# Fillers for TensorE at the head of a fused attention and two-layer kernel, with the order of the other work kept

## The chip, the core and the metric

The kernel runs on one core of a Trainium2 chip. The metric is device microseconds of one execution. Five engines work side by side, each in its own order: TensorE (matrix products, turns), VectorE, ScalarE and GpSimd (elementwise work), and SyncE, which here only issues DMA transfers. They wait for each other by semaphores.

## What is computed

Attention over 4 batches, 8 heads, 576 positions and 64 columns per head, with a rotation by position of q and k first; then two gated layers on the 2304 x 512 result. All in float32:

```python
q_rot, k_rot = rotate(q), rotate(k)            # x1*cos - x2*sin, x1*sin + x2*cos
scores = (1 / sqrt(64)) * q_rot @ k_rot.T
attn = exp(scores - max(scores)); attn /= attn.sum(-1) + 1e-9
x = (attn @ v), heads side by side              # 2304 x 512
h = (x @ w1) * (x @ w2) @ w3;  y = h @ w_out    # 512 -> 1024 -> 1024 -> 512
z = max(y @ v1, y @ v2, y @ v3) @ v_out         # 512 -> 768 -> 512
```

## The kernel before

The heads go in 16 pairs; the two heads of a pair, 64 columns each, fill the 128 partitions. For a pair, `prepare` (line 587) loads q and k with their swapped halves, multiplies them by the tables of cosines and sines, adds, and splits the result into a high and a low part of the tensor `st` (line 619), since most products are made of three products of parts in the faster float32r type. `prepare_v` does the same for the values. `score` (line 645) makes one block of scores of both heads: 12 products of 288 columns, or 6 for the block of the last 64 rows of both heads, which goes through one of two tiles `zs` that are zeroed at the start (line 582) and that pairs take in turn. Behind each block VectorE takes the row maximum (line 668) and ScalarE the exponential (line 671). `turn` (line 698) transposes blocks of 128 x 128 on TensorE by the identity matrix, which is loaded from DRAM into the tile `ident`; `fill` copies and subtracts the turned blocks into a high and a low part (lines 441 and 708), and `values` multiplies them with v. In the kernel before, the first instruction that reads `ident` is the first turn of pair 0.

Beside the pairs, weights that arrive as float64 words are loaded (`raw`), converted by ScalarE and VectorE (lines 506, 509, 511), and folded together (`fold`, plain float32 products); then the gates and the two layers follow, nearly all of it on TensorE.

Turns, values and folds take their PSUM banks from one set of four (`banks = Share(4)`): up to two tiles for turns, one for values, two for folds at a time.

The order of the work comes from a planner. Every piece is a task with an engine, a cost, a priority and its dependencies. `Plan.order` plays the tasks on a clock of its own, one per engine that starts at 0.7: of the tasks that are ready on an engine it takes the one with the least priority, lets the engine's clock wait for the task if it must, and adds the cost; loads have a modelled landing time. The order in which tasks are taken is the order in which their instructions are issued, engine by engine, and each engine runs its instructions in that order. The priorities written at each task are then shifted by 509 seeded random moves (`MOVES`), which also choose, where a task may run on either of two engines, which one.

Of the kernel before, what the change touches and what calls it, by code (L numbers as in the profile page):

```python
# [26 lines left out]

PN = (256, 320)
# [17 lines left out]
MOVES = (  # L46
# [50 lines left out]
def draws(seed):  # L97
    mask = (1 << 64) - 1
    s = (seed * 0xD1342543DE82EF95 + 1) & mask
    while True:  # L100
        s = (s + 0x9E3779B97F4A7C15) & mask
        z = ((s ^ (s >> 30)) * 0xBF58476D1CE4E5B9) & mask
        z = ((z ^ (z >> 27)) * 0x94D049BB133111EB) & mask
        yield z ^ (z >> 31)


def move(prio, pick, opts, place, seed):


    d = draws(seed)  # L110

    def uni():
        return (next(d) >> 11) * (1.0 / 9007199254740992.0)

    def stretch(parts):
        width = len(prio) / parts
        lo = uni() * (len(prio) + width) - width
        return lo, lo + width

    kind = next(d) >> 62  # L120
    if kind == 1:
        parts, share = (32, 128, 512, 2048)[next(d) >> 62], (0.03, 0.1, 0.3, 1.0)[next(d) >> 62]
        lo, hi = stretch(parts)
        for i in range(len(prio)):
            if opts[i] > 1 and lo <= place[i] < hi and uni() < share:
                pick[i] = int(uni() * opts[i])
        return
    if kind == 0:
        by, width = (0.3, 1.0, 3.0, 10.0)[next(d) >> 62], 1 << (next(d) >> 61)
        lo = int(uni() * (len(prio) + width)) - width  # L130
        x = uni() + uni() + uni() + uni() - 2.0
        for i in range(max(lo, 0), min(lo + width, len(prio))):
            prio[i] = prio[i] + by * 1.7 * x
        return
    by, share = (0.1, 0.3, 0.6, 1.5)[next(d) >> 62], (0.01, 0.03, 0.1, 0.3)[next(d) >> 62]
    parts = (1, 8, 32, 128)[next(d) >> 62]
    lo, hi = stretch(parts)
    if parts == 1:
        share *= 0.3
    for i in range(len(prio)):  # L140
        if lo <= place[i] < hi and uni() < share:
            x = uni() + uni() + uni() + uni() - 2.0
            prio[i] = prio[i] + by * 1.7 * x
# [1067 lines left out]
```

## Time and profile before

| | before |
|---|---|
| three runs | 926.47, 927.95, 928.65 us; median 927.95 |
| profiled execution, its own time | 927.38 us |
| its span, first to last instruction | 925.4 us |
| TensorE busy | 891.0 us (96%) |
| VectorE, ScalarE, GpSimd busy | 633.0, 475.9, 342.4 us |
| granted TensorE clock, mean | 0.998 |

Times in the rows are microseconds from the start of the span. PE is TensorE (PEld its loading of the stationary operand), DVE VectorE, ACT ScalarE, POOL GpSimd, SP SyncE, SPq its issuing of DMAs. A busy TensorE is not TensorE at its peak, since products are pipelined and their ends are modelled. L423 is the line of the product helper, L676 that of the turn, L444 that of the loads.

### The profile page before, as it was taken

What the parts mean: (1) busy time and instruction counts of PE and PEld (TensorE: products, weight loads), DVE (VectorE), ACT (ScalarE), POOL (GpSimd) and SP (SyncE); (2) the same over time, 40 slices, a digit from 0 to 9 for tenths busy, and PEclk for the clock granted to TensorE, in tenths of its full rate; (3) what the DMA queues carried; (4) which work ended last, traced back from release to release, by engine and by line L of the source; (5) the groups of instructions that cost most, each with busy time, mean ns of one, the idle gap of its engine ahead of it and who ended that gap; (6) DMA issues with size and microseconds to landing.
All of it is one profiled execution on the core that took longest, in us unless ns stands there. A gap on an engine that the chain in (4) does not pass through costs nothing.

```text
span 925.4 us, 16273 instructions
## 1 busy us (share of the span) xinstructions
PE 891.0 (96%) x5922; PEld 823.8 (89%) x5922; DVE 633.0 (68%) x1133; ACT 475.9 (51%) x1054; POOL 342.4 (37%) x332
## 2 busy tenths in 40 slices
PE   1898999999999999999999999999999999999998
PEld 1666769989999999999998999999999999999886
DVE  6997988898867677687766333657988577578300
ACT  4677887876757577567544222434323322334411
POOL 3645767766436366522110000433332333232000
PEclk9999999999999999999999999999999999999999
DMA  8454546542333123310147543323324114255511
GB/s 265 134 188 153 165 154 209 149 142 84 100 103 97 44 92 93 97 50 18 37 153 213 199 127 89 103 86 97 98 86 140 55 46 148 68 163 195 201 57 68
DMA packets 80287, 110.31 MB, mean 119 GB/s; under 512 B 27984, under 2 KB 61008, under 8 KB 80208
## 3 DMA queue, kind: packets, MB, share of 16 engines
q1 hardware_dynamic: 80208, 109.29, 37.4%
q8 instruction: 46, 0.75, 0.3%
q14 instruction: 33, 0.27, 0.1%
HBM read 83.76 MB, written 25.50 MB: 118 GB/s over the span
## 4 chain that ended last, share of the span: by engine, by line
PE 80%; DVE 9%; DMA 7%; issue 2%; ACT 1%; SPq 1%; POOL 0%; DVEq 0%; ACTq 0%
PE q L423 46%; PE m L423 15%; PE t L676 7%; PE pv L423 6%; PE s L423 6%; DVE pt L708 3%; DMA raw<-in_w3t_dram 3%; DVE sm L668 2%; DMA raw<-in_w_dram 2%; DVE raw L509 1%; DMA rawc<-in_w3t_dram 1%; SPq L444 1%; DMA vr<-in_vv_dram 1%; DVE cw L511 1%; ACT pt L441 0%
## 5 line engine op out<-in xcount | busy, mean ns | idle before, releaser
L708 DVE TENSOR_TENSOR pt<-t,pt 128x320 fp32r<-128x320 f32 (+3 forms) x256 | 132.4, 528 | 34.5 <-ACT pt L441 29.4
L441 ACT CAST pt<-t 128x320 fp32r<-128x320 f32 (+3 forms) x234 | 103.5, 456 | 51.9 <-PE t L676 24.9
L423 PE MATMUL pv<-pt,v 128*128 128x256 f32 (+1 forms) x576 | 113.2, 317 | 5.1 <-DVE pt L708 4.0
L668 DVE TENSOR_REDUCE sm<-s 128x1 f32<-128x576 f32 x144 | 103.9, 749 | 19.8 <-PE s L423 18.8
L423 PE MATMUL q<-gt,wp 128*128 128x384 f32 x576 | 100.0, 334 | 0.0
L423 PEld LDWEIGHTS q<-gt,wp 128*128 128x128 f32 x576 | 99.8, 188 | 0.0
L423 PEld LDWEIGHTS pv<-pt,v 128*128 128x128 f32 x576 | 82.8, 189 | 15.7 <-DVE pt L708 9.5
L423 PE MATMUL s<-st 64*128 64x288 f32 x768 | 71.7, 316 | 18.7 <-ACT st L618 11.7
L423 PEld LDWEIGHTS s<-st 64*128 64x128 f32 x768 | 55.6, 190 | 32.5 <-ACT st L618 11.7
L423 PE MATMUL q<-yc__7620,u 128*128 128x384 f32 x378 | 71.2, 340 | 0.0
L423 PE MATMUL q<-yc__7946,u 128*128 128x384 f32 x378 | 70.8, 340 | 0.0
L423 PE MATMUL q<-yc__7376,u 128*128 128x384 f32 x378 | 70.5, 340 | 0.0
L423 PEld LDWEIGHTS q<-yc__7946,u 128*128 128x128 f32 x378 | 67.1, 188 | 0.1
L423 PEld LDWEIGHTS q<-yc__7620,u 128*128 128x128 f32 x378 | 67.1, 188 | 0.0
L423 PEld LDWEIGHTS q<-yc__7376,u 128*128 128x128 f32 x378 | 67.1, 188 | 0.0
L441 ACT COPY tmp<-q 128x384 f32<-128x384 f32 x45 | 21.5, 479 | 84.7 <-PE q L423 84.5
L441 ACT COPY ga<-q 128x512 f32<-128x512 f32 (+2 forms) x34 | 16.9, 497 | 65.6 <-PE q L423 61.6
L1066 POOL TENSOR_TENSOR tmp<-tmp 128x384 f32<-128x384 f32 x20 | 22.6, 1132 | 72.3 <-ACT tmp L441 72.3
L423 PE MATMUL q<-tail,tail 128*128 128x512 f32 x216 | 49.1, 389 | 0.0
L423 PEld LDWEIGHTS q<-tail,tail 128*128 128x128 f32 x216 | 40.5, 188 | 8.4
L522 DVE TENSOR_TENSOR gt<-gt 128x768 fp32r<-128x768 f32 x24 | 26.7, 1117 | 25.3 <-ACT gt L521 25.3
L1079 DVE TENSOR_TENSOR tmp<-q,tmp 128x384 f32<-128x384 f32 x54 | 29.9, 554 | 15.4 <-PE q L423 15.2
(1222 smaller groups left out, 2050.9 us busy)
## 6 DMA issues: line engine op xcount, KB each, us to landing
gt<-g_d SPq DMA_DIRECT2D x24, 384.0 KB
raw<-in_m_dram SPq DMA_DIRECT2D x72, 128.0 KB
raw<-in_w_dram SPq DMA_DIRECT2D x16, 512.0 KB
h_d<-top SPq DMA_DIRECT2D x36, 192.0 KB
tail<-h_d SPq DMA_DIRECT2D x36, 192.0 KB
raw<-in_wo_dram SPq DMA_DIRECT2D x12, 512.0 KB
raw<-in_w3t_dram SPq DMA_DIRECT2D x12, 512.0 KB
g_d<-ga SPq DMA_DIRECT2D x32, 160.0 KB
```

The lines of the kernel that those rows point to most:

```text
L423: pe.matmul(o, a, b, start=start, stop=stop, **kw)
L441: (e.copy if e is act else e.tensor_copy)(o, i)
L444: return add("SP", .5, lambda: sync.dma_start(o(), src()), r, w, part, deps, prio, tail=us)
L509: add("DVE", 0.42, lambda: dve.tensor_scalar(low_word(), low_word(), 29, None, ALU.logical_shift_right), part=[raw], deps=raw.writers, pri ...
L511: add("DVE", 0.69, lambda: dve.scalar_tensor_tensor(u(), u(), 3, low_word(), ALU.logical_shift_left, ALU.bitwise_or), r=[raw], deps=[first ...
L522: either(sb(n, "DVE"), lambda on: on.tensor_tensor(sel()[:, LO], f32(sel()[:, LO]), f32(sel()[:, HI]), ALU.subtract), r=[dst], part=[dst], ...
L668: add("DVE", c_dve(S), lambda s=s, col=col: dve.tensor_reduce(sm.t[:, 0, col:col + 1], s.t[:, :, :288], axis=AX.XY, op=ALU.max, negate=Tru ...
L676: pe.transpose(o, x, ident.t)
L708: add("DVE", c_dve(n), lambda: dve.tensor_tensor(low(pt.t), src(t.t), f32(hi(pt.t)), ALU.subtract), r=[t], part=[pt], deps=[h], prio=prio)
L1066: either(sb(TN), lambda on: on.tensor_tensor(s5.t, s1.t, s5.t, ALU.add), r=[s1], w=[s5], prio=prio)
L1079: add("DVE", c_dve(TN), lambda: dve.tensor_tensor(e.t, at_(o), e.t, ALU.add), r=[accs[o]], w=[e], prio=prio)
```

## The change

- TensorE gets a task `early` of 22 plain float32 products of 128 x 128 x 128. They read the second `zs` tile, which a new memset fills with ones, and write a PSUM bank of their own; a further memset then sets the tile back to zero.
- Ahead of every TensorE task that finds a gap on the planner's clock, once that clock is past 10.0, the kernel issues turns of the identity into the same bank: 0.7 of the gap, divided by 0.109. This goes on until the last values product of pair 0 (`plan.last`, a task that issues nothing); until then the bank is held, one of the four. The turns cost nothing on the planner's clock.
- The moves are replaced by two tables: `PLACE`, one rank for each task, and `OTHER`, the tasks that take their second engine. Of the tasks that both kernels have, the ranks are those of the final priorities before. The four new tasks stand among them at 148 (ones), 27 (products), 293 (zeros) and 28 (the end).

```diff
--- before.py
+++ after.py
@@ -25,6 +25,7 @@
 FF = 1024
 EPS = 1e-9
 
+IDLE = 1
 PN = (256, 320)
 PO = (0, 256)
 TN = 384
@@ -43,108 +44,245 @@
 
 
 
-MOVES = (
-    10000024, 10000032, 10000048, 10000067, 10000110, 10000112, 10000169, 10000173, 10000183, 10000227, 10000237,
...
+PLACE = (
+    14, 15, 148, 27, 293, 16, 311, 24, 188, 258, 238, 259, 218, 256, 240, 118, 241, 216, 208, 198, 203, 129, 299,
...
 )
 
 
-def draws(seed):
...
-def move(prio, pick, opts, place, seed):
...
+OTHER = (
+    23, 24, 51, 60, 67, 146, 152, 155, 156, 188, 277, 286, 288, 348, 415, 417, 418, 527, 533, 556, 680, 800, 851,
...
+)
 
 
 class Task:
-    __slots__ = ("eng", "dur", "emit", "prio", "tail", "deps", "after", "out", "next", "fresh", "shared", "num", "lock", "opts")
+    __slots__ = ("eng", "dur", "emit", "prio", "tail", "deps", "after", "out", "next", "fresh", "shared", "num", "lock", "opts", "idle")
 
 
 class Buf:
@@ -184,6 +322,7 @@
     LAT = {"PE": 0.05, "ACT": 0.035, "DVE": 0.035, "POOL": 0.08, "SP": 0.1, "HOST": 0.0}
     LAP = {"PE": 0.0, "ACT": 0.1, "DVE": 0.08, "POOL": 0.04, "SP": 0.0, "HOST": 0.0}
     DRAIN = 0.165
+    HEAD, FILL = 22, 0.7
 
     def __init__(self):
         self.tasks, self.rings = [], []
@@ -200,7 +339,7 @@
         k.eng, k.dur, k.prio, k.tail = eng, dur, prio, tail
         k.lock = eng == "POOL" if lock is None else lock
         k.opts = [(eng, dur, k.lock)]
-        k.num, k.out, k.next = len(self.tasks), [], []
+        k.num, k.out, k.next, k.idle = len(self.tasks), [], [], 0
         need = set(deps)
         after, fresh = set(), []
         for b in r:
@@ -224,6 +363,7 @@
         k.shared = list({id(b): b for b in list(r) + list(w) + list(part) if b.ring.share}.values())
 
         def go():
+            self.ahead(k.idle)
             for b in fresh:
                 b.t = b.make(b.slot)
             emit()
@@ -250,6 +390,7 @@
         soon = {e: [] for e in clock}
         now = {e: [] for e in clock}
         dma, port, done = 0.0, 0.0, []
+        idle, idling = {}, True
         for k in tasks:
             if not left[k.num]:
                 heapq.heappush(soon[k.eng], (0.0, k.num))
@@ -286,6 +427,10 @@
                 live[b.ring] += 1
             if k.lock:
                 at = max(at, port)
+            if k is self.last:
+                idling = False
+            if e == "PE" and idling and clock[e] > 10.0:
+                idle[k] = max(0, int(self.FILL * (at - clock[e]) / 0.109))
             end = at + k.dur
             if k.lock:
                 port = end
@@ -319,7 +464,7 @@
                 left[o.num] -= 1
                 if not left[o.num]:
                     heapq.heappush(soon[o.eng], (ready[o.num], o.num))
-        return clock["PE"], done, slot
+        return clock["PE"], done, slot, idle
 
     def issue(self):
         for ring in self.rings:
@@ -338,16 +483,14 @@
                 d.out.append(k)
             for d in sorted(k.after, key=lambda d: d.num):
                 d.next.append(k)
-        prio = [k.prio for k in self.tasks]
-        place = {k.num: i for i, k in enumerate(self.order(prio)[1])}
-        pick = [0] * len(prio)
-        for seed in MOVES:
-            move(prio, pick, [len(k.opts) for k in self.tasks], place, seed)
+        other = set(OTHER)
         for k in self.tasks:
-            k.eng, k.dur, k.lock = k.opts[pick[k.num]]
-        best = self.order(prio)
+            k.eng, k.dur, k.lock = k.opts[k.num in other]
+        best = self.order(PLACE)
         for b, n in best[2].items():
             b.slot = n
+        for k, n in best[3].items():
+            k.idle = n
         for k in best[1]:
             k.emit()
 
@@ -451,6 +594,7 @@
     cw_r = ring(gap, [128, 512], F32, "cw", 2)
     banks = Share(4)
     m_r = ring(ps_m, [128, 512], F32, "m", 2, banks)
+    idle_r = ring(ps_m, [128, 512], F32, "idle", 1, banks)
     banks2 = Share(8)
     q_r = ring("ps2", [128, 512], F32, "q", 8, banks2, False)
     q2_r = ring("ps2", [128, 512], F32, "q", 8, banks2)
@@ -675,6 +819,23 @@
     def tr(o, x):
         pe.transpose(o, x, ident.t)
 
+    bank = idle_r.new()
+
+    def ahead(n):
+
+        for _ in range(n):
+            tr(bank.t[:, :128], ident.t)
+
+    def early():
+
+        for _ in range(plan.HEAD):
+            mm(bank.t[:, :128], f32(zs[1].t[:, 0]), f32(zs[1].t[:, 1]), True, True)
+
+    plan.ahead = ahead
+    add("POOL", 0.3, lambda: pool.memset(f32(zs[1].t), 1.0), part=[zs[1]], deps=zs[1].writers, prio=-1, lock=False)
+    plan.first = add("PE", 8.5, early, r=[zs[1]], w=[bank], prio=-9)
+    add("POOL", 0.3, lambda: pool.memset(f32(zs[1].t), 0.0), part=[zs[1]], deps=[plan.first], prio=0.5, lock=False)
+
     def inverse(p):
 
         sm, prio = sms[p], 2 * p + 2.3
@@ -801,6 +962,8 @@
         prepare(p)
         if p == 0:
             load(lambda: ident.t, lambda: cs[:, 2 * S:], 0.4, w=[ident], prio=-2)
+        if p == IDLE:
+            plan.last = add("PE", 0.0, lambda: None, r=[bank], deps=[vs[p - 1].users[-1]], prio=-9)
         sms[p], xs[p] = sm_r.new(), [r.new() for r in x_r]
         prepare_v(p)
         for part in range(2):
```

## Rows read from the trace of the kernel before

**Rows 1.** by stretch: each engine's busy us, granted TensorE clock, DMA share, GB/s

```profile
27.00:38.00 11.00, 8.73 (x65) 6.92 (x64) 10.81 (x20) 7.98 (x19) 5.42 (x4) 1.00 0.25 69
77.40:130.00 52.60, 51.46 (x326) 36.27 (x326) 45.01 (x84) 44.83 (x109) 33.07 (x28) 1.00 0.57 170
```

**Rows 2.** chain that ended last, by time: start us, us, what

```profile
20.26 1.59 PE s L423 x9
21.88 0.77 DVE sm L668
23.64 1.79 PE s L423 x6
25.46 0.76 DVE sm L668
36.78 5.48 DMA raw<-in_w3t_dram
77.42 0.55 PE t L676 x3
```

**Rows 3.** timeline of TensorE: start us, us, engine line op out<-in xcount

```profile
11.67 0.61 PE L423 MATMUL s<-st 64*128 64x288 f32 x2 [11.67 <-ACT st L618]
25.22 0.41 PE L676 MATMUL t<-ident,p__187 128*128 128x128 f32 x1
29.49 0.27 PE L676 MATMUL t<-ident,p__187 128*128 128x128 f32 x1
33.59 1.58 PE L423 MATMUL pv<-pt,v 128*128 128x256 f32 x9
38.30 0.37 PE L676 MATMUL t<-ident,p__283 128*128 128x128 f32 x1
40.39 0.63 PE L676 MATMUL t<-ident,p__236 128*128 128x128 f32 x2
46.24 1.06 PE L423 MATMUL s<-st,z__109 128*128 128x288 f32 x6 [1.22 <-ACT p__474 L671]
51.18 1.06 PE L423 MATMUL s<-st 64*128 64x288 f32 x12
60.86 4.56 PE L423 MATMUL m<-wo,w 128*128 128x512 f32 x10
```

**Rows 4.** timeline of SyncE's queue, the issue of the identity

```profile
8.71 1.24 SPq L444 DMA_DIRECT2D ident<-in_cs_dram  x1
```

**Rows 5.** DMA packets of 13:14, 14:15, 15:16, 16:17 and 16.75:17

```profile
DMA packets 121, 0.40 MB, mean 400 GB/s; under 512 B 11, under 2 KB 20, under 8 KB 121
DMA packets 716, 0.32 MB, mean 322 GB/s; under 512 B 585, under 2 KB 684, under 8 KB 716
DMA packets 674, 0.23 MB, mean 235 GB/s; under 512 B 645, under 2 KB 657, under 8 KB 674
DMA packets 140, 0.28 MB, mean 283 GB/s; under 512 B 75, under 2 KB 83, under 8 KB 140
DMA packets 35, 0.09 MB, mean 349 GB/s; under 512 B 16, under 2 KB 17, under 8 KB 35
```

**Rows 6.** by stretch of one us, columns as in the first group

```profile
38.00:39.00 1.00, 0.81 (x5) 0.81 (x6) 0.94 (x3) 0.26 (x1) 0.00 (x0) 0.67 1.00 379
41.00:42.00 1.00, 0.73 (x4) 0.52 (x3) 0.63 (x2) 1.00 (x5) 1.00 (x2) 0.63 1.00 377
```

**Rows 7.** timeline of GpSimd, VectorE and ScalarE

```profile
0.98 0.31 POOL L582 MEMSET z__109<- 128x256 f32 x1
14.99 1.41 DVE L668 TENSOR_REDUCE sm<-s 128x1 f32<-128x576 f32 x2
17.74 0.72 ACT L671 ACTIVATE p__187<-s,sm 128x576 f32<-128x576 f32 x1
18.75 0.72 ACT L638 CAST v<-vr 128x640 fp32r<-128x640 f32 x1 [0.20 <-DMA vr<-in_vv_dram]
37.47 0.42 DVE L441 COPY x__313<-pv 64x256 f32<-64x256 f32 x1
```

More of the change, by code (lines that the diff above doesn't have):

```diff
@@ L42 @@
 TERMS = ((HI, HI), (LO, HI), (HI, LO))
-MOVES = (
[47 rows of a table removed]
-)
-def draws(seed):
[L98 to L104, printed above, removed]
-def move(prio, pick, opts, place, seed):
[L110 to L143, printed above, removed]
+PLACE = (
[222 rows of a table added]
+)
+OTHER = (
[6 rows of a table added]
+)
 class Task:
-    __slots__ = ("eng", "dur", "emit", "prio", "tail", "deps", "after", "out", "next", "fresh", "shared", "num", "lock", "opts")
+    __slots__ = ("eng", "dur", "emit", "prio", "tail", "deps", "after", "out", "next", "fresh", "shared", "num", "lock", "opts", "idle")
 class Buf:
```

272 rows, old and new, of tables (MOVES, OTHER, PLACE) are left out of this document.

## The prediction

> **What bounds the kernel now.** I read the stretches first, then the chain of waits, then the timelines of the head. From 77.40 us on TensorE has hardly a gap (51.46 of 52.60 us), so whatever time the head takes is handed on to the end. Before that another engine sets the pace: from 27 to 38 VectorE is busy 10.81 of 11 us and TensorE 8.73 [rows 1]. The chain says the same in order of time: at the head it goes through the second scores (20.26, 1.59 us), a row maximum, the common scores (23.64, 1.79 us) and the next maximum at 25.46; from there VectorE runs without a gap until a weight load (36.78, 5.48 us) takes over, and at 77.42 the chain passes to TensorE [rows 2]. So TensorE sits on the path twice before 25.5 us, and then not until 77.4.
>
> At both places it runs at its lower level. The eight turns at 25.22 start 0.21 us apart and those at 29.49 start 0.11 apart; the common scores take 1.79 us there and 1.06 at 46.24, where the granted clock is 1.00 [rows 2, 3]. The profile's clock column shows no event before 38 us, so for the head the durations must be read. A second spell at 1.2 GHz is recorded: the clock column falls to 0.67 in 38:39 and is back to 0.63 in 41:42, where 0.5 would be all half; so it fell at 38.3 and rose at 41.7, some 3.4 us at half [rows 6].
>
> **The change part by part.**
>
> *The table.* PLACE ranks the tasks exactly as the final priorities of the kernel before do, with four new entries, and OTHER holds the engine choices. Durations and loads are the same. This part costs 0.
>
> *22 products of ones.* A third memset (0.31 us, as the one at 0.98 [rows 7]) lets them start at about 1.6 us. Ten halves of a 512-column product take 4.56 us at 1.00 [rows 3], so a half of 128 columns takes about 0.11, and 22 products of two halves 5.0 us at full, 10.0 at half clock: over between 6.6 and 11.6. The first scores wait for ScalarE until 11.67 [rows 3], so alone they cost nothing. The memset back to zero waits for them on GpSimd, whose next work comes after the first scores.
>
> *The turns.* The planner puts turns ahead of a TensorE task, 0.7 of the gap on its own clock over 0.109 us, once that clock is past 10.0. For the kernel before, that clock gives gaps of 4.45 us before the second scores, 2.12 before the common scores and 1.38 before the first turns, hence 28, 13 and 8 turns; some 50 more follow in smaller groups until pair 0 is done. The first scores are the case to look at. The planner has them at 14.70. The products end there at 1.69 + 8.5 = 10.19, which is over 10.0, so this gap of 4.51 us is open and 28 turns are placed in it. Each of them reads the identity, and TensorE takes its instructions in order.
>
> *When the identity is there.* It is issued on SyncE's queue at 8.71 [rows 4], behind twelve loads of tables, queries, keys and values and two weight loads of 512 KB. Its 64 KB are 128 rows of 512 bytes, and these are the only packets between 512 bytes and 2 KB in that time, so subtracting the "under 512 B" count from the "under 2 KB" count finds them: 9 in 13:14, 99 in 14:15, 12 in 15:16, 8 in 16:17, of which one after 16.75 [rows 5]. These are all 128. The identity is complete at about 17.0 us. In the kernel before nobody needs it until 25.0. In the changed kernel the first scores, which could start at 11.67, stand behind 28 turns that wait for 17.0.
>
> *What the 28 turns take.* At the spacings of 25.22 and 29.49 [rows 3]: 28 x 0.109 = 3.05 us all at full clock, 28 x 0.213 = 5.96 all at half. TensorE has then been idle for at least 5 us, so I let them begin at half; the nearest spell of turns at the low level lasted 3.4 us before the clock was back [rows 6]. Taking that length: 16 x 0.213 + 12 x 0.109 = 4.7 us. First scores at 21.7, over at 22.75 by the 1.06 us of 51.18 [rows 3].
>
> *What follows, step by step.* VectorE holds the first maxima at 14.99 (two, 1.41 us) and does nothing behind them until they are there [rows 7]. The first is done at 23.5, so the first exponential, 17.74 before [rows 7], starts at 23.5. From it to the second scores it was 2.52 us, 0.20 of them a wait for a values load [rows 2, 7] that has long landed; 2.32 remain: 25.8, which is also where the 28 turns before them (3.05 from 22.75) end. With 1.06 for the scores they are over at 26.9; before it was 21.85. The next step, maximum and exponential, is 1.76 as before (21.88 to 23.64 [rows 2]): common scores at 28.65, the 13 turns (1.42) fit ahead of them, and with 1.06 instead of 1.79 they end at 29.7; before it was 25.43. The head is **4.3 us late** there: 5.0 from the second scores less 0.7 from the faster common scores. The eight turns after it end about 4.5 late (29.7 + 1.7 against 26.9); VectorE has two weight steps to do before it needs them.
>
> *What lies behind.* From 25.46 VectorE is full and its weight loads are issued from its own releases, so lateness is passed on to 77.4 and by TensorE to the end. The second half-clock spell saves TensorE about 1.7 us (half of 3.4), but what is late there is the load of 36.78 [rows 2], so I book 0. The largest later group, 15 turns (1.6 us), stands before the values at 33.59, where the chip shows no gap [rows 3]; they end at 35.17 and VectorE reads the result at 37.47 [rows 7], which hides it; without that cover 1.6.
>
> *The bank.* One of four PSUM banks is held through pair 0. By the planner's clock four buffers overlap there at three points, so a few turns move behind a release. No row shows three banks. Lower bound -0.1 (a group of turns, 0.44, off VectorE's path), upper bound 1.0 (one step of copy and subtraction, about 0.6 and 0.6, late once). I take 0.2, near the lower end, because VectorE has work queued there.
>
> *Sum.* 927.38 (the profiled execution's own time) + 4.3 + 0.2 = 931.9. The median of the runs is 0.57 above that execution; forecast **932.2**.
>
> *Bounds.* All turns at full: first scores at 20.05 and every later step 1.7 earlier, +2.6. All of the first 28 at half: +5.5. An identity complete at 15, where 99 + 9 of 128 packets were in, takes up to 2 off. Together +0.6 to +6.5: 928.0 to 934.4.
>
> **A rule that speaks against the turns.** Twelve turns ran one after another, the first at 38.30 and the last two at 40.39, with two values products behind them [rows 3], and the clock rose at 41.7 [rows 6]. The Trainium skill, "TensorE: Matmul & The Clock Gate", Part 4 (PE-mode transpose), says that transposes don't count for the clock gate as other products do, so it doesn't open for them. By that rule the turns here would neither raise nor hold the clock. The spell of 38 to 42 speaks against it, and 25.22 decides nothing, as scores ran just before. By the rule the time would be that of the third rival; the sum above goes by the rows.
>
> **The rivals.**
>
> 1. *The turns don't hold the first scores* (not slower). If the identity were complete before about 8.6 us (11.67 less 3.05), or the gap before the first scores stayed unfilled, only the faster scores would be left: 0.53 at 20.26 and 0.73 at 23.64 [rows 2, 3], -1.3, so 926.6. For it: VectorE and ScalarE, not TensorE, set the steps between 14.99 and 20.26. Against it: the packets [rows 5], and that the identity is only issued at 8.71 [rows 4].
>
> 2. *The wait is short.* Identity complete at 15 and turns at full clock: +0.6 to +1.8, about 929. For it: 108 packets were in by 15; a few late ones may be one DMA engine's affair in one execution. Against it: two loads of 512 KB stand ahead of it.
>
> 3. *Turns at half clock throughout* (the rule of the Trainium skill's page named above). The clock does not rise for turns. First scores at 22.95, 1.7 long, 24.7; second scores behind 28 turns of 0.213 at 27.7 or 30.6, the later counts, over at 32.4; common scores behind 13 turns, 35.2 to 37.0, against 25.43: +11.5, so 939. Against it: the clock that came back behind turns [rows 6].
>
> 4. *More turns than gaps.* The chip's gaps after 27 us are small (TensorE 8.73 of 11 busy [rows 1]); if the cover of the later groups is gone and the bank costs its upper bound, 1.6 + 0.8 more: 934.6.
>
> **How the numbers follow.** Forecast 0.61, rival 1 0.11, rival 2 0.13, rival 3 0.06, rival 4 0.09. The likeliest one's own range is 930.0 to 934.4. What a measurement can tell from no change is about 0.2%, 1.9 us: faster is below 926.1, slower above 929.8. Rival 1 is split about evenly at 926.1; rival 2 is mostly within. Faster 0.07, same 0.16, slower 0.77. The range of 8 in 10 takes in rival 2 and rival 4 and leaves out rivals 1 and 3: 927.8 to 935.5.
>
> **What would show it.** In the profile after: 44 product halves from about 1.6 us; a gap in TensorE ended by the identity's load near 17; 28 turns; first scores at 20 to 23 where they were at 11.67; VectorE idle from about 15 to 22.8 before its first maximum; the maximum of 25.46 at 28 to 31; no half clock at 38 to 42; TensorE's full stretch beginning about 4 us later than 77.4. Wrong would be: first scores still near 11.7, or a gap of TensorE before 77 that takes the 4 us back.

## The result, and the profile after

| | before | after |
|---|---|---|
| median of five runs beside each other | 926.84 us (925.16 to 928.65) | 935.87 us (932.81 to 938.16) |
| ratio after to before | | 1.0089, 95% interval 1.0071 to 1.0107 |
| profiled execution, its own time | 927.38 us | 933.63 us |
| its span | 925.4 us | 931.8 us |
| TensorE busy | 891.0 us (x5922) | 907.5 us (x6095) |
| a second round of the change | 927.23 us (26 runs) | 934.60 us (5 runs), 1.0083 [1.0070, 1.0095] |

The change costs 0.8 to 0.9%, some 8 us; the forecast said 932.2 us, a ratio of about 1.005. Slower was right and the place was right; the size was too small, and 935.87 lies just over the upper end of the range.

TensorE's timeline of the changed kernel answers to [rows 3] (start us, us, what, and in brackets the idle time before it with what ended it):

```profile
1.71 6.68 PE L566 MATMUL idle<-z__109 128*128 128x128 f32 x44 [1.71 <-POOL z__109 L835]
15.50 4.74 PE L820 MATMUL idle<-ident 128*128 128x128 f32 x28 [7.10 <-DMA ident<-in_cs_dram]
20.17 1.06 PE L566 MATMUL s<-st 64*128 64x288 f32 x12
21.16 3.28 PE L820 MATMUL idle<-ident 128*128 128x128 f32 x28
24.36 1.06 PE L566 MATMUL s<-st 64*128 64x288 f32 x12
25.35 1.64 PE L820 MATMUL idle<-ident 128*128 128x128 f32 x13
27.23 1.06 PE L566 MATMUL s<-st,z__105 128*128 128x288 f32 x6 [0.24 <-ACT p__300 L815]
```

The products of ones are over at 8.39. Then TensorE does nothing for 7.10 us, until the identity lands; 28 turns follow, and behind them the first scores at 20.17, which stood at 11.67 before. From there to the common scores no score waits for ScalarE by more than 0.24 us, and each block takes 1.06 us, where the chain before held 1.59 us (nine of twelve products) and 1.79 [rows 2]: that gives part of the 8.5 us back. The common scores end 2.9 us late (28.29 against 25.43).

The chain of waits, which answers to [rows 2], now runs over the identity:

```profile
8.93 6.53 DMA ident<-in_cs_dram
15.50 4.74 PE idle L820 x28
20.24 1.03 PE s L566 x12
28.33 0.76 DVE sm L812
186.26 7.93 DMA raw<-in_w_dram
```

VectorE's timeline of the changed kernel, and below it GpSimd's, both around the step at which the head hands over:

```profile
21.26 1.42 DVE L812 TENSOR_REDUCE sm<-s 128x1 f32<-128x576 f32 x2 [6.52 <-PE s L566]
29.00 1.73 DVE L655 SCALAR_TENSOR_TENSOR wo<-wo,raw 128x512 uint32<-128x512 uint32 x1
30.65 1.64 DVE L653 TENSOR_SCALAR raw<-raw 128x512 uint32<-128x512 uint32 x1
```

```profile
26.88 3.30 POOL L763 TENSOR_TENSOR st<-early,st 128x576 fp32r<-128x576 f32 x2
```

The same two VectorE steps in the kernel before, and the GpSimd step that ran when the first of them began:

```profile
26.13 0.68 DVE L511 SCALAR_TENSOR_TENSOR wo<-wo,raw 128x512 uint32<-128x512 uint32 x1
26.73 1.64 DVE L509 TENSOR_SCALAR raw<-raw 128x512 uint32<-128x512 uint32 x1
24.83 1.40 POOL L612 TENSOR_TENSOR qk__177<-qk__177,tabs__107 128x576 f32<-128x576 f32 x1
```

The weight step `wo` took 0.68 us before and takes 1.73 now. It ends 0.55 us behind a GpSimd step that was running when it began (30.73 against 30.18), and in the kernel before 0.58 us behind one (26.81 against 26.23). In all profiles but that of experiment 3, 13 of them, it is 0.55 to 0.63 us, while the length of `wo` goes from 0.68 to 1.93: it is what was left of that GpSimd step, and some 0.6 us more. A late head is not needed for it; in experiment 10, where the head is not late, it took 1.60 us:

```profile
25.35 1.60 DVE L655 SCALAR_TENSOR_TENSOR wo<-wo,raw 128x512 uint32<-128x512 uint32 x1
25.00 1.40 POOL L756 TENSOR_TENSOR qk__215<-qk__215,tabs__107 128x576 f32<-128x576 f32 x1
```

In the change the lateness grows here from 2.87 us at the maximum (28.33 against 25.46) to 3.92 at the step behind (30.65 against 26.73).

By stretch (engines' busy us, granted clock, DMA share, GB/s), answering to [rows 1, 6], and one us in which the clock rises:

```profile
18.00:19.00 1.00, 1.00 (x9) 1.00 (x8) 0.00 (x0) 0.00 (x0) 0.00 (x0) 0.73 0.88 346
27.00:38.00 11.00, 9.44 (x78) 7.93 (x79) 10.75 (x16) 7.03 (x19) 9.31 (x6) 1.00 0.29 79
27.00:60.00 33.00, 30.07 (x241) 25.59 (x242) 30.82 (x55) 24.25 (x60) 22.06 (x17) 1.00 0.38 123
38.00:39.00 1.00, 1.00 (x11) 1.00 (x10) 1.00 (x2) 1.00 (x2) 0.33 (x1) 1.00 0.00 0
77.40:130.00 52.60, 49.73 (x307) 33.80 (x307) 45.59 (x81) 43.51 (x106) 34.23 (x29) 1.00 0.54 166
```

VectorE is as full as before from 27 to 38, so lateness can't be made good there. The half-clock spell of 38 to 42 is gone. TensorE lacks 1.7 us in the stretch 77.4 to 130 against before: its full stretch begins later (from 83.6 to 130 it is busy 45.27 of 46.40 us).

The table shows how late each kernel but that of experiment 3 runs: the start of an instruction less the start of the same instruction before, with columns by the time in the kernel before (VectorE's instructions up to 207, TensorE's from 520 on), in one profiled execution each. The profiled execution is not always near the median: 933.70 us against 929.42 with the first 28 turns left out, 937.00 against 932.81 for the wait alone, 929.87 against 931.16 for the products alone. So the last columns can differ by several us from the ratio.

| kernel | ratio, 95% interval | 26.7 | 49.5 | 83.0 | 207 | 520 on | us at half clock, 27 to 100 |
|---|---|---|---|---|---|---|---|
| change | 1.0089 [1.0071, 1.0107] | +3.9 | +4.1 | +4.3 | +6.1 | +6.4 | 0 |
| change, second round | 1.0083 [1.0070, 1.0095] | +5.7 | +6.4 | +5.5 | +6.5 | +7.3 | 0 |
| no fillers, bank free | 1.0006 [0.9993, 1.0019] | -0.6 | +0.3 | -1.3 | -1.2 | -0.6 | 6.8 |
| no fillers, bank held | 1.0019 [1.0007, 1.0031] | -0.2 | +1.3 | +0.4 | +0.8 | +1.0 | 3.4 |
| identity early, all fillers | 1.0022 [1.0011, 1.0033] | -0.7 | +0.2 | -0.8 | +0.6 | +0.9 | 0 |
| wait alone | 1.0069 [1.0043, 1.0096] | +3.6 | +7.7 | +9.1 | +9.4 | +9.6 | 17.1 |
| products, 28 turns | 1.0122 [1.0104, 1.0140] | +6.6 | +7.1 | +10.6 | +12.8 | +13.1 | 16.2 |
| first 28 turns left out | 1.0037 [1.0022, 1.0051] | +2.3 | +3.6 | +4.9 | +6.2 | +6.4 | 3.4 |
| products alone | 1.0050 [1.0037, 1.0063] | -0.8 | -0.2 | +0.5 | +0.8 | +2.6 | 0 |
| late turns alone | 1.0045 [1.0029, 1.0061] | -0.3 | +1.3 | +3.8 | +4.9 | +5.7 | 3.4 |
| identity early, head only | 1.0022 [1.0009, 1.0035] | +1.2 | +1.7 | +3.2 | +3.5 | +4.0 | 6.8 |
| ones in all head gaps | 1.0032 [1.0017, 1.0047] | +0.1 | +0.4 | +2.1 | +3.1 | +3.9 | 6.8 |

Of the last 2 us of the change 1.5 come at 188: a weight load issued at 186.26 takes 7.93 us (chain above), and VectorE waits 2.17 us for it. The same load in the kernel before, and below it in experiment 5, whose head is not late:

```profile
181.68 6.41 DMA raw<-in_w_dram
180.87 7.79 DMA raw<-in_w_dram
```

Experiment 5 loses 1.4 us there (0.8 early at 180.7, 0.6 late at 188.1), so it doesn't take a late head for this load to be long.

### The profile page after: what moved, and what is told of

Read it like the earlier page. It is cut to its first block, busy times and chain, and to the rows that moved or that the text cites. A ratio compares the mean times of both kernels' runs of the same rounds, so it can differ in the third digit from the quotient of the medians.

```text
span 931.8 us, 16621 instructions
## 1 busy us (share of the span) xinstructions
PE 907.5 (97%) x6095; PEld 840.2 (90%) x6095; DVE 636.2 (68%) x1133; ACT 476.4 (51%) x1054; POOL 345.0 (37%) x334
## 4 chain that ended last, share of the span: by engine, by line
PE 81%; DVE 9%; DMA 5%; ACT 2%; issue 2%; SPq 0%; DVEq 0%; ACTq 0%
PE q L566 48%; PE m L566 14%; PE t L820 7%; PE pv L566 6%; PE s L566 6%; DVE pt L869 3%; DMA raw<-in_w_dram 3%; DVE sm L812 2%; DMA raw<-in_w3t_dram 1%; DVE raw L653 1%; ACT pt L584 1%; DVE cw L655 1%; DMA ident<-in_cs_dram 1%; PE idle L820 1%; DMA qk__142<-in_qk_dram 1%
## 5 line engine op out<-in xcount | busy, mean ns | idle before, releaser
L566 PE MATMUL s<-st 64*128 64x288 f32 x768 | 68.1, 308 | 0.0
L566 PEld LDWEIGHTS s<-st 64*128 64x128 f32 x768 | 53.1, 184 | 12.7 <-issue 6.7
L584 ACT COPY tmp<-q 128x384 f32<-128x384 f32 x45 | 21.6, 479 | 84.0 <-PE q L566 83.7
```

Source lines behind the costliest of these rows:

```text
L566: pe.matmul(o, a, b, start=start, stop=stop, **kw)
L584: (e.copy if e is act else e.tensor_copy)(o, i)
```

## The experiments

Each was timed in five rounds against the kernel before. All but the third keep the change's table of ranks. While the bank is held, TensorE's order differs from the kernel before in one place: two values products, at 48.84 before, stand ahead of six turns instead of behind them. The kernels that give the bank back early (the second of experiment 4, and 9 and 10) have the order before everywhere, fillers apart.

**1. The first 28 turns left out** (`e1_no_head_turns`).

```diff
-            if e == "PE" and idling and clock[e] > 10.0:
+            if e == "PE" and idling and clock[e] > 11.0:
```

> The changed kernel without the 28 turns of the identity ahead of the first scores; the 22 products and all later turns stay. Theory A (the first scores stand behind the identity's load and 28 turns): first scores back at about 11.7 us, the faster scores at 20.3 and 23.6 give 1.3 back, so 925 to 926.5, a ratio to before of 0.998 to 1.000. Rival B (the later turns or the held PSUM bank cost): still 930 or more, and the lateness appears after 27 us. Rival C (the clock): scores at 12 and 20 still at half clock, since the products end at 8.4 and TensorE is idle for 3 us; then no gain, ratio 1.000 to 1.002.

929.42 us, 1.0037 [1.0022, 1.0051]. More than half of the loss goes, not all of it as theory A had it; the wait moved one step on: the 28 turns before the second scores are now the first readers of the identity.

```profile
12.68 0.61 PE L566 MATMUL s<-st 64*128 64x288 f32 x2 [4.20 <-ACT st L762]
16.41 6.05 PE L820 MATMUL idle<-ident 128*128 128x128 f32 x28 [1.12 <-DMA ident<-in_cs_dram]
22.40 1.07 PE L566 MATMUL s<-st 64*128 64x288 f32 x12
```

The first scores start at half clock (two of them in 0.61 us), although 6.77 us of products ended 4.2 us before them.

**2. Products of ones alone** (`e2_products_only`).

```diff
-    HEAD, FILL = 22, 0.7
+    HEAD, FILL = 22, 0.0
```

> The 22 products of ones alone, no turn of the identity anywhere, the PSUM bank still held. Theory A: no loss, 926 to 927.5; the first scores at 11.7 perhaps at full clock, later ones at half again as in the kernel before, so within 0.1% of before. Rival B (the bank costs): as slow as the changed kernel less its turns, 929 or more. Rival C: as A.

931.16 us, 1.0050 [1.0037, 1.0063]. In the head they cost nothing (0.8 us early at 26.7, as without fillers) and gain nothing, since the clock has fallen again before the first scores. The whole time is nevertheless above that of no fillers, and above the forecast; the profiled execution, the shortest of the five, shows the drift only from 207 on. Its cause stays open.

**3. The identity asked for first, as a planner's task** (`e3_ident_early`).

```diff
-        best = self.order(PLACE)
+        best = self.order([-1 if k is self.ident else PLACE[k.num] for k in self.tasks])
...
-            load(lambda: ident.t, lambda: cs[:, 2 * S:], 0.4, w=[ident], prio=-2)
+            plan.ident = add("ACT", 0.1, lambda: act.dma_start(ident.t, cs[:, 2 * S:]), w=[ident], prio=-2, tail=0.4)
```

> The changed kernel with the identity loaded first, from ScalarE's queue, instead of behind two weight loads; all 129 turns stay. Theory A: the products end at 8.4, the 28 turns follow at full clock and end at 11.5, first scores at 11.7 at full clock; 1.3 us less than before from the faster scores, 925 to 926.5, ratio 0.997 to 1.000. Rival B (it is the turns themselves, not what they wait for): first scores at 11.7 but 929 or more. Rival C (the turns don't open the clock): the 28 turns take 6 us, first scores at 14.4, 928.

954.03 us, 1.0300 [1.0281, 1.0320]: a miss of the experiment. With the task's engine and landing time changed, the planner took a large part of the other tasks in another order, so this says nothing of the identity. It was done again as experiment 5.

**4. No fillers at all** (`e4_no_fillers`), the bank still held through pair 0; **and with the bank given back at once** (`e8_bank_free`).

```diff
-    HEAD, FILL = 22, 0.7
+    HEAD, FILL = 0, 0.0
```

and for the second, besides:

```diff
-            plan.last = add("PE", 0.0, lambda: None, r=[bank], deps=[vs[p - 1].users[-1]], prio=-9)
+            plan.last = add("PE", 0.0, lambda: None, r=[bank], deps=[plan.first], prio=-9)
```

> Neither products nor turns, but the tables, the two further memsets and the held PSUM bank of the change. Theory A: as before, ratio 0.999 to 1.001. Rival B (the bank, or another order): part of the 9 us stays, 929 or more, with the timeline late from the first turn that waits for a bank.

> No fillers, and the PSUM bank is given back at once; the tables and the two memsets stay, so this is the kernel before but for two memsets. If the +1.7 of the run with no fillers comes from the held bank: ratio 0.999 to 1.001, no wait of a turn for VectorE of 1.7 us at 41. If it comes from the tables or is chance of the executions: 1.001 to 1.003 again.

928.70 us, 1.0019 [1.0007, 1.0031], and 928.29 us, 1.0006 [0.9993, 1.0019]. The table of ranks therefore costs nothing that can be measured. The held bank comes out at about 0.0013, 1.2 us, but the intervals overlap, so the times don't show that the bank alone makes this difference. In the profiles a place can be seen. TensorE's timeline with the bank held, a group of turns that waits for VectorE's subtraction to release a bank:

```profile
39.02 0.38 PE L820 MATMUL t<-ident,p__239 128*128 128x128 f32 x2
41.11 0.48 PE L820 MATMUL t<-ident,p__286 128*128 128x128 f32 x1 [1.71 <-DVE pt L869]
```

With the bank free all twelve turns run in one piece, the last at 38.97, and it is a product that waits:

```profile
38.97 0.38 PE L820 MATMUL t<-ident,p__239 128*128 128x128 f32 x2
40.86 0.56 PE L566 MATMUL pv<-pt,v 128*128 128x320 f32 x2 [1.51 <-DVE pt L869]
```

By 49.5 the one is 1.3 us late, the other 0.3.

**5. The identity's load issued ahead of everything on ScalarE's queue** (`e7_ident_early`), all 129 turns and 22 products kept, in the same order.

```diff
-                b.t = b.make(b.slot)
+                if b.t is None:
+                    b.t = b.make(b.slot)
...
+        self.start()
         for k in best[1]:
             k.emit()
...
-    plan.ahead = ahead
+    def start():
+        ident.t = ident.make(ident.slot)
+        act.dma_start(ident.t, cs[:, 2 * S:])
+
+    plan.ahead, plan.start = ahead, start
...
-            load(lambda: ident.t, lambda: cs[:, 2 * S:], 0.4, w=[ident], prio=-2)
+            add("SP", 0.5, lambda: None, w=[ident], prio=-2, tail=0.4)
```

> The changed kernel with every task in its place and all 129 turns, but the identity's 64 KB issued from ScalarE's queue before anything else, so that it is there at about 3 us. (The earlier version of this also moved other work.) Theory A (lateness comes from the first 28 turns standing behind the identity's load): turns from 8.3 to 11.4 at full clock, first scores at 11.7 to 12.5, no TensorE gap ended by the identity; 5 to 8 us better than the changed kernel. What the held bank costs (+1.7 with no fillers) stays: 927 to 929, ratio 1.000 to 1.002. Rival B (the number of turns, wherever they stand): 931 or more. Rival C (turns don't keep the clock): first scores at 14.5, 931.

929.12 us, 1.0022 [1.0011, 1.0033]; the change beside it on the same chip (`after_again`) 934.60 us, 1.0083 [1.0070, 1.0095]. The difference, 0.0061 or 5.7 us, is the wait with what it draws behind it. TensorE's timeline with the early identity:

```profile
8.79 3.22 PE L822 MATMUL idle<-ident 128*128 128x128 f32 x28
12.35 0.40 PE L568 MATMUL s<-st 64*128 64x288 f32 x2 [0.34 <-ACT st L764]
19.45 1.59 PE L568 MATMUL s<-st 64*128 64x288 f32 x11 [1.59 <-ACT p__240 L817]
20.98 2.67 PE L822 MATMUL idle<-ident 128*128 128x128 f32 x13
23.41 1.04 PE L568 MATMUL s<-st,z__107 128*128 128x288 f32 x6
```

The turns fill exactly the gap that they were meant for, and the first scores run at full clock at 12.35. But the second scores then wait for ScalarE as before, and behind this wait the granted clock is at half from 19.7 to 23.1: the 13 turns take 2.67 us, where the change had 1.64, and the common scores start behind them at 23.41, later than with no turns (22.95 and 22.50 in experiment 4), and take 1.04 us instead of 1.78. The head ends 0.7 us early, where it ended 0.2 to 0.8 early with no turns at all (experiments 2 and 4). A faster TensorE is worth next to nothing there.

**6. The change again** (`after_again`).

> The changed kernel once more, for a second profile and times beside the others. If the length of the half-clock spell at the head sets the spread (931.0 to 936.3 of span at clock 0.996 to 0.992): a profile with a spell longer than 6.8 us has the first scores after 20.2 and a span of over 933; one with the same spell has 931 to 932.

Besides the time above, its timeline shows how the size varies between executions:

```profile
1.72 8.13 PE L566 MATMUL idle<-z__109 128*128 128x128 f32 x44 [1.72 <-POOL z__109 L835]
16.05 5.96 PE L820 MATMUL idle<-ident 128*128 128x128 f32 x28 [6.20 <-DMA ident<-in_cs_dram]
21.95 1.06 PE L566 MATMUL s<-st 64*128 64x288 f32 x12
29.01 1.06 PE L566 MATMUL s<-st,z__105 128*128 128x288 f32 x6 [0.23 <-ACT p__300 L815]
```

The identity is 0.55 us later and all 28 turns run at half clock, 5.96 us instead of 4.74; so the scores come 1.78 us later, and 1.78 is also the difference at 26.7 in the table. The recorded half-clock spell is 6.8 us long in both (11.7 to 18.5 in the first profile, 14.8 to 21.6 in this one), so it was not its length, which the expectation named, but its place that made the turns longer. In the profiles of experiments 1 and 8, too, the 28 turns behind the wait took 6.05 and 6.22 us.

**7. The wait alone** (`e5_wait_only`): no products, and a single turn ahead of the first scores.

```diff
-    HEAD, FILL = 22, 0.7
+    HEAD, FILL = 0, 0.0
...
-                idle[k] = max(0, int(self.FILL * (at - clock[e]) / 0.109))
+                idle[k] = 0 if idle else 1
```

**8. Products and the 28 first turns** (`e6_head_turns_only`), without the 101 turns behind them.

```diff
-                idle[k] = max(0, int(self.FILL * (at - clock[e]) / 0.109))
+                idle[k] = 0 if idle else max(0, int(self.FILL * (at - clock[e]) / 0.109))
```

> No products, and a single turn of the identity ahead of the first scores instead of 129 turns; the PSUM bank is held as in the change. It separates the wait for the identity from the length of the 28 turns behind it. Theory A (wait and length both count, the wait being partly hidden): first scores at 15.7 to 17.2 at half clock, over at 17.4 to 18.9, VectorE's first maximum 2.4 to 3.9 late, but ScalarE waits for other loads until 18.7 anyway, so the second scores are 0 to 1.5 late; with the bank's +1.7 a ratio of 1.002 to 1.0035. Rival B (the wait alone is the loss): 1.007 to 1.009 as the change.

> The change with its 22 products and the 28 turns ahead of the first scores, but none of the other 101 turns; the bank is held. Theory A (the first 28 turns carry the loss): ratio 1.006 to 1.009, first scores at 20 to 22. Rival B (the second group of 28 and the later ones carry a good part): 1.003 to 1.005.

932.81 us, 1.0069 [1.0043, 1.0096], and 938.21 us, 1.0122 [1.0104, 1.0140]. Waiting alone takes more than was expected of it, near what its rival B had, though its six runs spread from 929.84 to 937.75; and the shorter list of turns costs more than the whole, more than either theory had. Timeline of the first:

```profile
17.32 0.48 PE L820 MATMUL idle<-ident 128*128 128x128 f32 x1 [17.32 <-DMA ident<-in_cs_dram]
17.73 1.81 PE L566 MATMUL s<-st 64*128 64x288 f32 x12
25.98 1.78 PE L566 MATMUL s<-st,z__105 128*128 128x288 f32 x6 [1.57 <-ACT p__223 L815]
```

and of the second:

```profile
16.68 6.22 PE L820 MATMUL idle<-ident 128*128 128x128 f32 x28 [7.91 <-DMA ident<-in_cs_dram]
30.23 1.81 PE L566 MATMUL s<-st,z__105 128*128 128x288 f32 x6 [1.48 <-ACT p__272 L815]
```

In both the clock is at half for the common scores (1.78 and 1.81 us) and again later. By stretch, the first and then the second (the granted clock is the number before the DMA share):

```profile
27.00:60.00 33.00, 26.03 (x157) 21.45 (x157) 28.91 (x46) 20.10 (x50) 17.76 (x15) 0.79 0.35 111
77.00:92.00 15.00, 14.10 (x80) 9.38 (x78) 10.95 (x19) 9.61 (x24) 9.58 (x8) 0.89 0.48 157
```

```profile
27.00:60.00 33.00, 25.72 (x176) 20.84 (x177) 30.00 (x51) 23.50 (x56) 22.13 (x17) 0.86 0.38 120
77.00:92.00 15.00, 11.98 (x58) 8.50 (x58) 9.34 (x15) 7.81 (x19) 9.93 (x8) 0.77 0.48 164
```

The change has 1.00 in 27:60. So the later turns, which the forecast booked as harmless, seem to give something back once the head is late: about 0.0035, 3.2 us (1.0122 against 1.0083 and 1.0089). That it comes from holding TensorE at 2.4 GHz is shown only in part. In experiment 8, 0.9 to 2.7 us are already in the first scores (22.83 against 21.95 and 20.17), the spell at 26 to 36 adds nothing (6.6 us late at 25.5, 6.8 at 38.6), and 2.5 us come between 74.8 and 83.0 (8.1 to 10.5), beside a spell at 84.2 to 91.0 that lies far behind the last turn of the change (53.58). In experiment 7 a spell does lie on the chain, from 46.8 to 57.1: between 45.1 and 49.5 that run goes from 4.6 to 7.7 us late, where the two profiles of the change lose 1.1 and 0.4.

**9. The early identity with head turns only, bank given back before the first needed turn** (`e9_head_only`), and **10. products of ones in place of the turns in the three head gaps** (`e10_ones`), both tries at a version that gains.

```diff
-            plan.last = add("PE", 0.0, lambda: None, r=[bank], deps=[vs[p - 1].users[-1]], prio=-9)
+            plan.last = add("PE", 0.0, lambda: None, r=[bank], deps=[plan.tasks[69]], prio=-9)
```

and for the tenth, besides, without the early identity:

```diff
-        for _ in range(n):
-            tr(bank.t[:, :128], ident.t)
+        for _ in range(n // 2):
+            mm(bank.t[:, :128], f32(zs[1].t[:, 0]), f32(zs[1].t[:, 1]), True, True)
...
+            plan.tasks[4].deps.add(plan.tasks[69])
```

> As the run with the early identity, but the fillers end with the common scores (22 products, 28 + 28 + 13 turns) and the PSUM bank is given back before the first turn that is needed. Theory A with the bank as a second cost: all of the loss gone and the faster scores left, -1.3, 925 to 926.5, ratio 0.998 to 1.000. Rival B (fillers slow what runs beside them): 928 or more.

> A version meant to beat both: products of ones in place of turns (14, 14 and 6 ahead of the first, second and common scores), which need no identity, nothing afterwards, and the PSUM bank given back before the first needed turn. Theory A: no wait for the identity, scores at full clock, -0.7 to -1.3 at the head: ratio 0.9985 to 1.000. Rival B (a faster TensorE at the head is hidden by loads and VectorE): 1.000 to 1.002. Rival C (products end at 8.4 and the clock falls before the first scores): as B.

929.57 us, 1.0022 [1.0009, 1.0035], and 930.69 us, 1.0032 [1.0017, 1.0047]. Both miss their theory A. Neither gains, so none of the versions tried beats the kernel before: the first scores are at full clock in both, and the head ends no earlier than without fillers. Both have a half-clock spell near 80 us, where the kernel before has none; beside it they lose 1.7 us (+1.6 to +3.2 between 74.8 and 83.0 in experiment 9, where the change, at full clock, loses 0.7).

**11. The later turns alone** (`e11_late_turns`): the 60 from the first needed turns on, bank held.

```diff
-    HEAD, FILL = 22, 0.7
+    HEAD, FILL = 0, 0.7
...
-            if e == "PE" and idling and clock[e] > 10.0:
+            if e == "PE" and idling and clock[e] > 24.0:
```

> Only the later turns of the identity stay, those from the first needed turn of the first pair on (60 of them, where the whole change has 129); no products of ones, no turn ahead of the first, second or common scores. The accumulator that the fillers write stays held as in the change. Nothing waits for the identity before the kernel before does. Theory A (the loss of the change is the wait of the 28 turns for the identity and their length, and the later turns give a part back by holding the clock): the run is no later than the run without fillers (1.0019), by 0 to 2 us better, so a ratio of 0.9995 to 1.002; no half-clock stretch between 30 and 60 us, where the run with turns only ahead of the first scores had one at 26 to 36. Rival B (turns only add work to TensorE, and the later ones lengthen the path too): 1.002 to 1.004, 0.5 to 2 us above the run without fillers.

931.85 us, 1.0045 [1.0029, 1.0061]: rival B, if anything above its upper end. The clock was indeed full from 28.8 to 80, and this did not help: eight turns at half clock ahead of the first needed ones make VectorE 1.0 us later there (0.3 early at 28.3, 0.6 late at 30.2), and at 49.5 the run is as late as without fillers and with the bank held (+1.3). The rest comes later, in the chain of waits from a load issued at 69.55, and behind it from a half-clock spell that the idle TensorE fell into:

```profile
24.35 1.91 PE L820 MATMUL idle<-ident 128*128 128x128 f32 x8
69.55 8.23 DMA raw<-in_w3t_dram
77.81 0.66 ACT L650 ACTIVATE w<-raw 128x512 f32<-128x512 f32 x1 [1.99 <-DMA raw<-in_w3t_dram]
80.25 1.78 PE s L566 x6
```

It is the second of a pair of loads. In the kernel before the second was issued at 67.84 and ScalarE used it 6.6 us later:

```profile
74.48 0.68 ACT L506 ACTIVATE w<-raw 128x512 f32<-128x512 f32 x1 [0.21 <-DMA raw<-in_w3t_dram]
```

So holding the clock did not pay where the head is on time. Whether the turns lengthened that load or it was this execution's alone can't be told from one profile.

## Why the prediction was right in its mechanism and short in its size

*The table*, booked 0: right, 1.0006 with an interval over 1.

*The products*, 5.0 to 10.0 us, over between 6.6 and 11.6: 6.68 and 8.13 us, over at 8.4 and 9.9, hidden in the head. That they cost something in the whole (experiment 2) was not foreseen and is not explained.

*The identity at 17.0*: 15.50, 16.05, 16.41, 16.68 and 17.32 in the five profiles in which TensorE waited for it. Counting its packets in the trace before found the wait that decides; experiment 5 removed it, and 5.7 us with it.

*The 28 turns*, 3.05 to 5.96, taken 4.7: 4.74 in the profile of the result, but 5.96, 6.05 and 6.22 in the three others with 28 turns behind the wait, nearly all at half clock. So the 4.7 met the shortest of four, which is luck; against the others this term was mis-sized by 1.3 to 1.5. The clock rises behind turns alone: nothing else ran on TensorE from 15.50 on, and it is granted in full from the middle of 18:19 (0.73 in that us). By this the third rival has fallen. The rule of the Trainium skill, "TensorE: Matmul & The Clock Gate", Part 4 (PE-mode transpose), that transposes don't engage the gate's full level, does not hold for these turns of float32; the measurement decides.

*The head, +4.3*: +3.9 and +5.7 at the weight step, 4.8 in the mean. In the first profile the sum was near by two errors that cancel, which is luck. The common scores ended 2.9 late, not 4.3, because the identity was 1.5 us earlier; and 1.05 us came on top where VectorE's `wo` step grew from 0.68 to 1.73, which no term held. In the second the identity was 0.95 earlier, the turns 1.3 longer, and the same `wo` step made it 5.7.

*Passed on to the end*: right for the head's share, wrong as a whole. The forecast read the stretch 77.4 to 130 as full and stopped there. Between 83.0 and the end the lateness still grew by 2.1 and 1.8 us in the two profiles of the change; in the first, the weight load at 186.26 holds 1.5 of it. TensorE still waits for VectorE's loads there. The late head does not explain this growth: from 26.7 to the end it is 2.4 and 1.6 us in the change, and 1.6 with the early identity (0.7 early, then 0.9 late).

*The bank, 0.2 of -0.1 to 1.0*: probably mis-sized. About 1.2 us by the times of experiment 4, with intervals that overlap, and 1.6 us between the ends of its two profiles; in the profiles turns stand behind a release, the place that the upper bound named.

*Half clock, booked 0*: the spell of 38 to 42 is gone, as said. That executions differ by such spells was not weighed. The five runs of the change show mean granted clocks of 0.996 and 0.996 for 933.63 and 932.81 us, and 0.994, 0.992 and 0.994 for 938.16, 936.62 and 935.87: the profiled execution is one of the first two, and the median is one of the others. This is not the whole spread: the second round has 0.996 in four of its five runs, for 934.44 to 935.62 us.

Together: 4.5 forecast for the profiled execution, 6.25 measured there. The last step of the forecast, 931.9 and 0.57, makes 932.5 and not 932.2. In the ratios of the second round the loss is 7.7 us: 5.7 go with the wait (experiment 5), and of the 2.0 that are left the held bank may hold about 1.2; the rest, and the 0.6 us by which the first round is above the second, stay without a shown cause. Rivals 1 and 2 fell with the wait of 7.10 us, though the identity of rival 2, at 15, was nearer to the 15.50 measured than the forecast's 17.0. Rival 4's first part, cover gone for the later turns, is not what was seen in 27 to 60; its bank part may be.

## What to carry to other kernels

A filler takes its place in the engine's order: before it is issued, ask which operand it reads and when that lands, since everything behind it waits with it. Filler work belongs where its only operands are already on chip (experiment 10 had them so, and still lost 0.3%), and it can pay only where the engine that it keeps fast is the one that ends the step; here ScalarE and VectorE did, and first scores at full clock gained nothing. When lateness is passed down a chain, follow it to the end of the trace, since a stretch that looks full still has waits; and before you blame the late start for what is lost there, look at a version that starts on time: here it met the same longer load.

## What the runs showed of the hardware

Turns of the identity in float32 can raise TensorE's clock and hold it: it was granted in full within the 28 turns that began at 15.50, and stayed so with 101 more in the gaps, while with none there (experiment 8) it was at 0.86 in 27:60. They don't hold it through every wait: with the same 129 turns in experiment 5 it was at half from 19.7 to 23.1, behind a wait of 1.59 us. A VectorE step with two operands of 128 x 512 32-bit words, begun while GpSimd's elementwise step ran, ended 0.55 to 0.63 us behind that step in 13 of 13 profiles, and took 0.68 to 1.93 us by what was left of it.
